# First batch element: second-layer results leave PSUM by ScalarE and are added by GpSimd, its output is sent in parts, and x's first products go ahead of its second half's transposes

## The chip, the cores and the metric

The kernel runs on one core of a Trainium2 chip. The metric is the device time of one execution in microseconds, the median of three runs; the profile is one more execution with the hardware profiler. Five engines work side by side, each in the order of its own instruction stream: TensorE (PE) multiplies, VectorE (DVE), ScalarE (ACT) and GpSimd (POOL) do elementwise work, SyncE (SP) issues DMA transfers. Semaphores connect them: an instruction that waits for another engine holds up everything behind it on its own engine. Matrix products land in PSUM banks; here a pool of two banks ("M") takes the products of the MLP part, a pool of four ("S") the attention scores.

## What is computed

Attention with normalized queries and keys, and its output, head by head side by side, goes through an MLP mixer. There are eight batch elements, 12 heads of 64, 448 positions, so x is 448 x 768 for each element.

```python
def _attn_ref(q, k, v, g_q, g_k):
    def rmsnorm(x, g):
        rms = np.sqrt(np.mean(x * x, axis=-1, keepdims=True) + 1e-06)
        return x / rms * g
    q_n, k_n = (rmsnorm(q, g_q), rmsnorm(k, g_k))
    scores = np.matmul(q_n, k_n.transpose(0, 1, 3, 2)) / np.sqrt(q.shape[-1])
    attn = np.exp(scores - np.max(scores, axis=-1, keepdims=True))
    attn = attn / (np.sum(attn, axis=-1, keepdims=True) + 1e-09)
    return np.matmul(attn, v)

def _moe_ref(x, w_tok1, w_tok2, w_ch1, w_ch2):
    xt = x.transpose(0, 2, 1)
    h = np.maximum(xt @ w_tok1, 0.0) @ w_tok2      # token mixing, 448 -> 256 -> 448
    u = x + h.transpose(0, 2, 1)
    h2 = np.maximum(u @ w_ch1, 0.0) @ w_ch2        # channel mixing, 768 -> 1536 -> 768
    return u + h2
# x = attention's output, (B,H,S,D) -> (B,S,H*D)
```

## The kernel before

The core works through the batch elements one after the other. While PE does the MLP of element b, the attention of element b + 1 is woven between its products, so PE always has two streams. Element 0 is special in its channel mixing. For the elements after it, the kernel uses seven products of half-size blocks instead of eight (Strassen's way), and needs sums of weight blocks for that. For element 0 the weights are only just being read from memory and converted, so it uses plain products, stage by stage, as the converted chunks come: 18 stages of the first layer, then 18 of the second (three output groups m = 2, 0, 1 of six stages each). The sums of weight blocks are made at the same time on GpSimd and written back to device memory (`ws`), to be read as "units" later. Each weight chunk takes four DVE operations, one ACT operation and two loads.

The stage of element 0's channel mixing:

```python
def first_stage(n):
    w, _, m, t = stages[n]
    wide = w is moe_w_ch2                       # second layer
    last = (KF if wide else KC) - 1
    if t == 0:
        st["m", 0], st["m", 1] = m_tile(), m_tile()        # both banks of pool M
    a, u = st.pop(("stage", n)), st["uT", 0]
    for o in range(2):
        ps = st["m", o][:, 0:S]
        for half in range(2):
            nc.tensor.matmul(out=ps, lhsT=a[:, o + 2 * half, :],                  # L781
                rhs=natural(half)[:, :, t, :] if wide else u[:, half * KC + t, :],
                start=(t == 0 and half == 0), stop=(t == last and half == 1))
        if t < last:
            continue
        if wide:
            to = u[:, o * KC + m, :]
            nc.vector.tensor_tensor(out=to, in0=to, in1=ps, op=ALU.add)           # L789
        else:
            nc.scalar.activation(out=natural(o)[:, :, m, :], ..., func=AF.Relu)
```

The matrix u is held transposed (`uT`). A result leaves by a DVE transpose of 32 x 32 blocks into one of four buffers, and four DMA transfers from SyncE's queue:

```python
turn_pool = pool("turn_pool", 4)

def trans_y(b, cc):
    t = st["y", cc] = turn_pool.tile([P, S], F32, name="turned")
    nc.vector.transpose(out=t[:], in_=st["uT", b][:, cc, :])                      # L900

def turns(b, cs, send=True):
    def one(cc):
        trans_y(b, cc)
        if send:
            later(2.0, lambda: send_y(b, cc, st.pop(("y", cc))))
    return [(0.3, lambda cc=cc: one(cc)) for cc in cs]

def y_order(b):        # for b = 0: 2, 5, 0, 3, 1, 4
    return [o * KC + m for m in ((0, 1, 2) if b else (2, 0, 1)) for o in range(2)]
```

`later` puts a piece of work a given number of (planned) microseconds further back in program order. Numbers such as 0.3 are weights by which `merge` weaves lists of work into one order; they are no measured times.

x of element 0 is turned by PE itself (`x_items`, L663, and an ACT copy, L665); `tok1` is the first product of token mixing on one half of x (L685, then `h`, L688), `tok2` the second (L693, then a DVE add into uT, L698). For later elements x goes through device memory: DVE transposes (L671), transfers to `xs` (L639) and back (L646). The loop:

```python
for b in range(B):
    early, double = middle_items(b)
    if b == 0:
        early, last = first_items(x_items(0, 1) + tok1_items(0, 0) + tok1_items(0, 1) + early, double, some)
    else:
        if in_next(b - 1):                       # every b but the first
            y, z = sends(b - 1, y_order(b - 1)[:4]), left
            left = [y[0], y[1], z[0], y[2], z[1], y[3]]
        run(merge(tok1_items(b, 0), left[:2]))
        begin, early = merge(tok1_items(b, 1) + early[:3 * KC], left[2:]), early[3 * KC:]
        # [...]
    att = ...                                    # attention of element b + 1, x_items(b + 1, 0) within
    if b == 0:
        last = x_items(1, 1) + merge(
            last, direct + sums[:5], turns(b, y_order(b)[:4], not in_next(b)))
    else:
        # [...]
    run(merge(att, early) + last)
    if b == 0:
        load_units(0)
    left = turns(b, y_order(b)[4:])
```

So four of element 0's six results are turned after the last conversions and stay in the four buffers; they are sent in the course of element 1, between the turns of the last two. `sums` and `direct` are the weight sums on GpSimd (L205 to L208), with loads L241 and stores L212; `unit` loads are L740; L177 loads raw weights, L264 to L309 convert them (L275 on ACT).

Of the kernel before, what the change touches and what calls it, by code (L numbers as in the profile page):

```python
# [13 lines left out]
ALU = mybir.AluOpType  # L14
# [12 lines left out]
def merge(*lists):  # L27

    totals = [sum(c for c, _ in l) or 1.0 for l in lists]
    done = [0.0] * len(lists)  # L30
    at = [0] * len(lists)
    res = []
    while True:
        live = [i for i in range(len(lists)) if at[i] < len(lists[i])]
        if not live:
            return res
        i = min(live, key=lambda i: (done[i] + lists[i][at[i]][0] / 2) / totals[i])
        c, fn = lists[i][at[i]]
        at[i] += 1
        done[i] += c  # L40
        res.append((c, fn))
# [3 lines left out]
def whole(ctx, tc, shifted, pre, q, k, v, g_q, g_k, moe_w_tok1, moe_w_tok2, moe_w_ch1, moe_w_ch2, out):  # L45


    nc = tc.nc
# [18 lines left out]
    KC, KF = NC // 2, NF // 2  # L67
# [47 lines left out]
    def later(us, fn):  # L115

        at = clock[0] + us
        i = len(pending)
        while i and pending[i - 1][0] > at:
            i -= 1  # L120
        pending.insert(i, (at, fn))
# [190 lines left out]
    def weight_items(lo, hi):  # L312

        def one(i):
            if 3 <= i and i + 2 < len(chunks):
                weight_load(i + 2)
            convert_bits(i - 2)
            if i < len(chunks):
                convert_first(i)
            if 0 <= i - 1 < len(chunks):  # L320
                convert_second(i - 1)
            if 0 <= i - 2 < len(chunks):
                convert_last(i - 2)
            if 0 <= i - 3 - len(first):
                store(i - 3 - len(first))
        return [(1.0, lambda i=i: one(i)) for i in range(lo, hi)]
# [298 lines left out]
    def send_y(b, cc, t):  # L625

        dst = out[b][:, cc * P:(cc + 1) * P]
        for i in range(0, P, 32):
            (nc.sync if in_next(b) else nc.scalar).dma_start(
                out=dst[:, i:i + 32].rearrange("(n t) c -> t n c", t=32),  # L630
                in_=t[i:i + 32].rearrange("t (n c) -> t n c", c=32))
# [22 lines left out]
    def trans_x(b, j):  # L654

        half, o = divmod(j, KC)
        if b == 0:

            if o == 0:
                x_tile(b, half)  # L660
            ps = s_tile("t_ps")
            for c in range(NS):
                nc.tensor.transpose(  # L663
                    ps[0:R, c * P:(c + 1) * P], st["uT", b][:, j, c * R:(c + 1) * R], ident[:, :])
            nc.scalar.copy(  # L665
                out=st["x", b, half][0:R, o], in_=ps[0:R, :].rearrange("p (c n) -> p c n", c=NS))
            return

        if j == 0:
            st["xt"] = tu_pool.tile([P, 2, KC, S], F32, name="xt", tag="tu")  # L670
        nc.vector.transpose(out=st["xt"][:, half, o, :], in_=st["uT", b][:, j, :])  # L671
        if o == KC - 1:
            t = st["xt"][:, half].rearrange("p j s -> p (j s)")
            if half:
                st.pop("xt")
            later(2.0, lambda: send_x(b, half, t))
            later(12.0, lambda: load_x(b, half))

    def tok1(b, jc, h):
        cs = slice(h * HC, (h + 1) * HC)  # L680
        if h == 0:
            st["h1", jc] = h1_pool.tile([P, C], F32, name="h1", tag="h1")
        ps = m_tile()
        for c in range(NS):
            nc.tensor.matmul(  # L685
                out=ps[:, 0:HC], lhsT=w1_sb[0:R, c, jc * P:(jc + 1) * P], rhs=st["x", b, h][0:R, :, c, :],
                start=(c == 0), stop=(c == NS - 1))
        nc.scalar.activation(out=st["h1", jc][:, cs], in_=ps[:, 0:HC], func=AF.Relu)  # L688
# [63 lines left out]
    def r_tile(i):  # L752
        return r_pool.tile([P, 2 * HS], F32, name=f"r{i}")
# [12 lines left out]
    def natural(o):  # L766
        s = (HB["B11"], HB["T1"]) if o == 0 else (HB["B21"], HB["B22"])
        return hb[:, s[0]:s[1] + 1:s[1] - s[0]]

    def first_stage(n):  # L770

        w, _, m, t = stages[n]
        wide = w is moe_w_ch2
        last = (KF if wide else KC) - 1
        if t == 0:
            st["m", 0], st["m", 1] = m_tile(), m_tile()
# [4 lines that stand above are left out]
                nc.tensor.matmul(  # L781
                    out=ps, lhsT=a[:, o + 2 * half, :],
                    rhs=natural(half)[:, :, t, :] if wide else u[:, half * KC + t, :],
                    start=(t == 0 and half == 0), stop=(t == last and half == 1))
            if t < last:
                continue
            if wide:
                to = u[:, o * KC + m, :]
                nc.vector.tensor_tensor(out=to, in0=to, in1=ps, op=ALU.add)  # L789
            else:  # L790
                nc.scalar.activation(
                    out=natural(o)[:, :, m, :], in_=ps.rearrange("p (i n) -> p i n", i=2), func=AF.Relu)
        st["used"].add(("stage", n))
# [104 lines left out]
# [12 lines that stand above are left out]
    def y_order(b):  # L910

        return [o * KC + m for m in ((0, 1, 2) if b else (2, 0, 1)) for o in range(2)]

    def sends(b, cs):
        return [(0.3, lambda cc=cc: send_y(b, cc, st.pop(("y", cc)))) for cc in cs]
# [3 lines left out]
    def x_items(b, h):  # L919
        return [(0.1, lambda j=j: trans_x(b, j)) for j in range(h * NC // 2, (h + 1) * NC // 2)]  # L920

    def tok1_items(b, h):
        return [(us(NS, HC), lambda j=j, h=h: tok1(b, j, h)) for j in range(NJ)]
# [13 lines left out]
    def in_next(b):  # L937


        return b < B - 1 and not shifted  # L940

    def first_items(tok, prods, some):


        convert = weight_items(BEFORE, len(chunks) + 3)
        items = merge(tok, convert[:5])
        for j, it in enumerate(prods[:-6]):
            items.append(it)
            items += [(0.0, convert[5 + k][1]) for k in range(len(convert) - 5) if begins(k) == j]
            if j % 2 and j < 2 * len(some):  # L950
                items.append(some[j // 2])
        return items, prods[-6:]

    def begins(k):


        return 2 + -(-k * 14 // 10) if k < 10 else min(k + 7, 29)
# [30 lines left out]
    for p in (4, 5):  # L988
# [7 lines left out]
        out=g_t[:, 0:1], in0=g_t[:, 0:1], scalar=float(D) ** 0.5, in1=g_t[:, 1:2],  # L996
# [19 lines left out]
    for b in range(B):  # L1016
        early, double = middle_items(b)
        if b == 0:
            early, last = first_items(x_items(0, 1) + tok1_items(0, 0) + tok1_items(0, 1) + early, double, some)
        else:  # L1020
            if in_next(b - 1):

                y, z = sends(b - 1, y_order(b - 1)[:4]), left
                left = [y[0], y[1], z[0], y[2], z[1], y[3]]
            run(merge(tok1_items(b, 0), left[:2]))
            begin, early = merge(tok1_items(b, 1) + early[:3 * KC], left[2:]), early[3 * KC:]
            if b == 1:
                early, double = merge(begin + early, sums[5:20]), merge(double, sums[20:])
                begin = []
            early = begin + early + double  # L1030
            early, last = early[:-4], early[-4:]
        lo = (b + AHEAD) * per + 1
        att = []
        if b + AHEAD < B:
            att = att_items(lo, lo + 10) + x_items(b + AHEAD, 0) + att_items(lo + 10, lo + per)
        if b == 0:
            last = x_items(1, 1) + merge(
                last, direct + sums[:5], turns(b, y_order(b)[:4], not in_next(b)))
        else:
            if b + 1 < B:  # L1040
                last = merge(last, x_items(b + 1, 1))
            last += last_items(b)
# [4 lines that stand above are left out]
# [187 lines left out]
def kernel(  # L1234
# [33 lines left out]
    with arm.Else():  # L1268
        whole(tc, True, pre, *args)
# [30 lines left out]
```

## Time and profile before

| | |
|---|---|
| time, median of 3 (lowest to highest) | 1353.59 us (1351.46 to 1354.92) |
| span of the profiled execution | 1351.2 us |
| PE, DVE, ACT, POOL busy | 95%, 56%, 27%, 28% of the span |
| tok1 of element 1 begins, of element 2, of element 3 | 274.4, 443.7, 601.5 us |
| L781, matmuls of element 0's channel mixing | 288, 539 ns each as listed (they overlap) |
| L789, the add out of PSUM, 128 x 448 | 6, 612 ns each |
| L900, output turns, all elements | 48, 636 ns each |
| L629, output transfers | 192, 56 KB each |

The page gives the busy share of each engine in 40 slices, the costliest groups of instructions, and the chain of work that ended last. The timeline gives one line for each run of instructions on an engine: start and length in us, engine, source line, operation, output and input by the program's names, shape and count, and in brackets the idle time before it with what ended it. A DVE wait that no PE instruction ever meets costs nothing; idle time of PE is what adds to the span.

### The profile page before, as it was taken

Reading aid. Unit: us, or ns where it says so; the run is one execution under the profiler, and the core shown is the slowest. Engines: PE = TensorE matmul, PEld = TensorE weight load, DVE = VectorE, ACT = ScalarE, POOL = GpSimd, SP = SyncE. Lnnn points to the kernel's source line nnn. Section 1 sums busy time; section 2 is a strip of 40 time slices with the busy share of each in tenths; the row PEclk is TensorE's granted clock in tenths of the full one; section 3 lists DMA queues with packets and bytes.
Section 4 is the critical chain, followed back from the end, with each engine's and each line's share of the span. In section 5 each row is a group of like instructions: output and inputs, shape, how many; then the busy total and the mean of one; then the engine's idle time right before and its main releaser. Section 6 shows DMA issues by size and latency. Waiting matters only on the chain.

```text
span 1351.2 us, 20151 instructions
## 1 busy us (share of the span) xinstructions
PE 1284.4 (95%) x7408; PEld 925.0 (68%) x7408; DVE 753.5 (56%) x1295; ACT 366.2 (27%) x734; POOL 380.4 (28%) x443
## 2 busy tenths in 40 slices
PE   5989997979999999999999999999999999999997
PEld 3444443436778577795778757795777967787997
DVE  6878689626664455635655265644556365543212
ACT  5553432122330233203331223302332023300100
POOL 1201540336652232202231123312322034211220
PEclk9999998989999999999999999999999999999998
DMA  9655487889879566694559665594665955475554
GB/s 209 164 169 150 127 222 198 185 228 228 220 197 237 131 168 158 136 246 99 134 147 203 169 148 127 133 255 91 168 158 127 249 118 157 124 178 136 184 168 99
DMA packets 501521, 227.82 MB, mean 169 GB/s; under 512 B 373605, under 2 KB 463077, under 8 KB 501413
## 3 DMA queue, kind: packets, MB, share of 16 engines
q1 hardware_dynamic: 488290, 224.60, 67.4%
q10 hardware_dynamic: 12994, 1.84, 0.8%
q8 instruction: 61, 1.00, 0.3%
q14 instruction: 48, 0.39, 0.1%
q0 software_dynamic: 128, 0.00, 0.0%
HBM read 186.84 MB, written 39.52 MB: 168 GB/s over the span
## 4 chain that ended last, share of the span: by engine, by line
PE 76%; DVE 11%; DMA 5%; SPq 2%; ACT 2%; POOL 2%; issue 2%; DVEq 0%; ACTq 0%; POOLq 0%
PE m_ps L864 25%; PE m_ps L807 19%; PE o_ps L459 8%; PE s_ps L385 8%; PE m_ps L781 7%; PE m_ps L685 5%; PE m_ps L693 3%; DVE es L427 2%; DVE qk_t L350 2%; DMA unit<-ws 2%; PE d_ps L439 1%; ACT e L389 1%; DVE uT L698 1%; DVE qkT L365 1%; PE m_ps L439 1%
## 5 line engine op out<-in xcount | busy, mean ns | idle before, releaser
L864 PEld LDWEIGHTS m_ps<-hb,unit 128*128 128x128 f32 x1764 | 332.1, 190 | 14.8 <-issue 11.3
L864 PE MATMUL m_ps<-hb,unit 128*128 128x224 f32 x1764 | 339.5, 354 | 1.1 <-DMA unit<-ws 1.1
L807 PE MATMUL m_ps<-tu,unit 128*128 128x224 f32 x1008 | 202.8, 356 | 3.9 <-DVE r L812 3.8
L807 PEld LDWEIGHTS m_ps<-tu,unit 128*128 128x128 f32 x1008 | 188.3, 190 | 23.0 <-DVE r L812 6.2
L389 ACT ACTIVATE e<-s_ps 128x448 f32<-128x448 f32 x336 | 156.8, 547 | 99.7 <-PE s_ps L385 99.1
L807 PE MATMUL m_ps<-uT,unit 128*128 128x224 f32 x756 | 155.0, 357 | 6.3 <-ACT r L828 3.1
L807 PEld LDWEIGHTS m_ps<-uT,unit 128*128 128x128 f32 x756 | 140.4, 190 | 23.2 <-DVE uT L698 7.0
L459 PE MATMUL o_ps<-e,v 64*64 64x448 f32 x1316 | 149.4, 541 | 0.1
L385 PE MATMUL s_ps<-qkT 64*64 64x448 f32 x1260 | 145.1, 547 | 0.2 <-ACT qkT L368 0.2
L873 POOL TENSOR_TENSOR uT<-uT,r 128x448 f32<-128x448 f32 (+1 forms) x56 | 52.7, 951 | 263.3 <-DVE r L873 150.0
L812 DVE TENSOR_TENSOR r<-m_ps,r 128x448 f32<-128x448 f32 x63 | 39.0, 619 | 124.1 <-PE m_ps L807 64.5
L873 DVE TENSOR_TENSOR uT<-uT,m_ps 128x448 f32<-128x448 f32 (+1 forms) x70 | 34.0, 502 | 124.6 <-PE m_ps L864 124.6
L427 DVE TENSOR_TENSOR es<-es,e 128x896 f32<-128x896 f32 x84 | 93.0, 1107 | 14.5 <-ACT e L389 11.2
L459 PEld LDWEIGHTS o_ps<-e,v 64*64 64x64 f32 x1316 | 49.7, 133 | 69.7 <-issue 64.9
L812 POOL TENSOR_TENSOR hb<-r,r 128x448 f32<-128x448 f32 x21 | 27.9, 1326 | 239.6 <-ACT r L828 181.3
L385 PEld LDWEIGHTS s_ps<-qkT 64*64 64x64 f32 x1260 | 44.0, 132 | 70.0 <-issue 60.6
L693 PE MATMUL m_ps<-w_sb,h 128*128 128x448 f32 x192 | 79.9, 560 | 12.5 <-ACT h L688 7.1
L685 PE MATMUL m_ps<-x,w_sb 112*128 112x384 f32 x256 | 87.1, 494 | 0.0
L427 POOL TENSOR_TENSOR es<-e 128x896 f32<-128x896 f32 x21 | 43.9, 2088 | 138.5 <-ACT e L389 138.5
L368 ACT ACTIVATE qkT<-qkT,g_t 128x448 f32<-128x448 f32 x36 | 24.1, 668 | 210.7 <-DVE qkT L365 210.7
L685 PEld LDWEIGHTS m_ps<-x,w_sb 112*128 112x128 f32 x256 | 48.4, 192 | 36.4 <-ACT e L389 4.2
L693 PEld LDWEIGHTS m_ps<-w_sb,h 128*128 128x128 f32 x192 | 35.5, 194 | 53.8 <-issue 24.4
(116 smaller groups left out, 1381.4 us busy)
## 6 DMA issues: line engine op xcount, KB each, us to landing
unit<-ws SPq DMA_DIRECT2D x294, 384.0 KB, 4.0
raw<-in_moe_w_ch_dram SPq DMA_DIRECT2D x72, 256.0 KB, 3.5
v<-in_v_dram SPq DMA_DIRECT2D x94, 112.0 KB, 4.3
xs<-xt SPq DMA_DIRECT2D x56, 168.0 KB, 4.4
x<-xs SPq DMA_DIRECT2D x14, 672.0 KB, 6.8
out_dram<-turned SPq DMA_DIRECT2D x168, 56.0 KB, 2.0
qk_t<-in_q_dram SPq DMA_DIRECT2D x144, 56.0 KB, 3.0
qk_t<-in_k_dram SPq DMA_DIRECT2D x144, 56.0 KB, 3.4
```

Of the source, the lines that this page charges most:

```text
L350: nc.vector.tensor_tensor(out=x, in0=x, in1=r.unsqueeze(2).to_broadcast(list(x.shape)), op=ALU.mult)
L385: nc.tensor.matmul(out=pss[i][rows_of(i, a), 0:S], lhsT=qkT[h, 1, k * D:(k + 1) * D], rhs=qkT[h, 0, :], start=True, stop=True)
L389: nc.scalar.activation(out=e[:, i, :], in_=pss[i][:, 0:S], func=AF.Exp)
L427: eng.tensor_tensor(out=es[:], in0=(es if k > 1 else st["e", t, 0])[:], in1=st["e", t, k][:], op=ALU.add)
L459: nc.tensor.matmul(out=st["o", p][a * D:(a + 1) * D, 0:S], lhsT=vt[rows, k * D:(k + 1) * D], rhs=e[rows, :], **kw)
L685: nc.tensor.matmul(out=ps[:, 0:HC], lhsT=w1_sb[0:R, c, jc * P:(jc + 1) * P], rhs=st["x", b, h][0:R, :, c, :], start=(c == 0), stop=(c == N ...
L693: nc.tensor.matmul(out=ps[:, 0:S], lhsT=st["h1", jc][:, cc * P:(cc + 1) * P], rhs=w2_sb[:, jc].rearrange("p c r -> p (c r)"), start=(jc == ...
L781: nc.tensor.matmul(out=ps, lhsT=a[:, o + 2 * half, :], rhs=natural(half)[:, :, t, :] if wide else u[:, half * KC + t, :], start=(t == 0 an ...
L807: nc.tensor.matmul(out=ps[:, j * HS:(j + 1) * HS], lhsT=w[:, t, j, :], rhs=m, start=(t == 0), stop=(t == KC - 1))
L812: add = lambda e, o, x, y: e.tensor_tensor(out=o, in0=x, in1=y, op=ALU.add)
L864: nc.tensor.matmul(out=ps[:, j * HS:(j + 1) * HS], lhsT=st["w"](j, t), rhs=hb[:, HB[what], t, :], start=(t == 0), stop=(t == KF - 1))
L873: add = lambda e, o, x, y: e.tensor_tensor(out=o, in0=x, in1=y, op=ALU.add)
```

## The change

Three things, all in batch element 0. The six adds of the second layer's results, which read PSUM on DVE, become a copy on ACT out of PSUM (into buffers that later elements use for their block products) and an add on GpSimd from there. This is to give the two banks back without waiting for DVE, which is converting weights. The output is sent in parts: two results are turned and sent while the last stages still run, the next two behind them, and the last two as before at element 1's beginning, where no sends of the first four are left. This is to keep the four turn buffers free. And the first product of token mixing on x's first half goes ahead of the transposes of x's second half, which wait for the attention of later heads.

```diff
@@ first_stage
             if wide:
-                to = u[:, o * KC + m, :]
-                nc.vector.tensor_tensor(out=to, in0=to, in1=ps, op=ALU.add)
+                to, c = u[:, o * KC + m, :], r_tile(1 + o)[:]
+                nc.scalar.copy(out=c, in_=ps)
+                nc.gpsimd.tensor_tensor(out=to, in0=to, in1=c, op=ALU.add)
@@ first_items: the list of stages j, with their conversions
             if j % 2 and j < 2 * len(some):
                 items.append(some[j // 2])
+            if j in (26, 28):
+                items += turns(0, [y_order(0)[j // 2 - 13]])
@@ the loop over elements
         if b == 0:
-            early, last = first_items(x_items(0, 1) + tok1_items(0, 0) + tok1_items(0, 1) + early, double, some)
+            early, last = first_items(
+                tok1_items(0, 0) + x_items(0, 1) + tok1_items(0, 1) + early, double, some)
         else:
-            if in_next(b - 1):
+            if b > 1 and in_next(b - 1):
                 y, z = sends(b - 1, y_order(b - 1)[:4]), left
@@
         if b == 0:
-            last = x_items(1, 1) + merge(
-                last, direct + sums[:5], turns(b, y_order(b)[:4], not in_next(b)))
+            last = x_items(1, 1) + merge(last, direct + sums[:5], turns(b, y_order(b)[2:4]))
```

What it does to the order of instructions: on PE, one group of four transposes, the first product, eight scores, four values, the second product, then twelve transposes, instead of sixteen transposes first. The second layer's chunks are 18 to 35. On ACT, the first two copies stand behind the conversion step of chunk 29, the next two behind that of chunk 35, the last two behind one square more. On DVE, one turn stands just before chunk 35's conversion begins, one behind chunk 34's last step, then four in a row behind x's transposes for element 1. On GpSimd, four adds stand ahead of the six weight sums made straight from staged chunks, and two behind the second of the sums whose chunks are read back from device memory.

## The prediction, made before the run

> **What bounds the kernel now.** I read the page's slices first. TensorE (PE) is busy 95% of the span, so a change that touches only batch element 0 can win no more than the holes in PE's row:
>
> ```profile
> PE   5989997979999999999999999999999999999997
> ...
> DVE  6878689626664455635655265644556365543212
> ...
> DMA  9655487889879566694559665594665955475554
> ```
>
> A slice is 33.8 us. Counted from 0, the holes lie in slices 2, 6 and 8 (68 to 101, 203 to 236 and 270 to 304 us); after that PE is dense. In slice 6 VectorE (DVE) is at 9 tenths; in slice 8 it is at 2 and the DMA engines at 8. PE in order of time, around these holes (start, length, engine, line, operation; at the end the idle time and its releaser):
>
> ```profile
> 84.91 1.08 PE L663 MATMUL t_ps<-ident,uT 128*112 128x128 f32 x8
> 87.68 0.65 PE L663 MATMUL t_ps<-ident,uT 128*112 128x128 f32 x4 [1.68 <-DVE uT L505]
> 91.81 1.10 PE L663 MATMUL t_ps<-ident,uT 128*112 128x128 f32 x4 [3.49 <-DVE uT L505]
> 92.71 3.80 PE L685 MATMUL m_ps<-x,w_sb 112*128 112x384 f32 x8
> ...
> 217.83 6.28 PE L781 MATMUL m_ps<-hb,stage 128*128 128x448 f32 x16
> 231.63 7.83 PE L781 MATMUL m_ps<-hb,stage 128*128 128x448 f32 x16 [7.52 <-DVE uT L789]
> ...
> 256.28 18.31 PE L781 MATMUL m_ps<-hb,stage 128*128 128x448 f32 x48 [1.43 <-DVE uT L789]
> ...
> 299.36 6.59 PE L693 MATMUL m_ps<-w_sb,h 128*128 128x448 f32 x12 [7.14 <-ACT h L688]
> ```
>
> Four holes: A, 5.2 us, the transposes of x's second half wait for attention of the last head pairs; B, 7.5 us, and C, 1.4 us, the second layer's next output group waits until DVE has added the last one out of its two PSUM banks; D, 7.1 us, element 1's token mixing waits for a ScalarE (ACT) result. Each long hole costs more than its idle time: the 16 matmuls behind B take 7.83 against 6.28 us, the 8 behind A 3.80 against 2.85 at 98.86, and behind D the table of stretches shows a granted clock of 0.85 from 300 to 310, another 1.5 us. A to D are 21.2 us idle and about 4 us of slow matmuls.
>
> What DVE, ACT and SyncE do at B, C and D (their timelines):
>
> ```profile
> 225.91 2.28 DVE L427 TENSOR_TENSOR es<-es,e 128x896 f32<-128x896 f32 x2
> ...
> 230.96 1.14 DVE L789 TENSOR_TENSOR uT<-uT,m_ps 128x448 f32<-128x448 f32 x2
> ...
> 237.74 1.16 DVE L365 STREAM_TRANSPOSE qkT<-qk_t 128x448 f32<-128x448 f32 x2
> ...
> 241.93 0.43 DVE L264 TENSOR_SCALAR e_t<-raw 128x512 uint32<-128x512 uint32 x1 [2.46 <-DMA raw<-in_moe_w_ch_dram]
> ...
> 296.14 0.65 DVE L900 STREAM_TRANSPOSE turned<-uT 128x448 f32<-128x448 f32 x1 [20.89 <-DMA out_dram<-turned]
> ...
> 298.82 0.49 ACT L688 ACTIVATE h<-m_ps 128x384 f32<-128x384 f32 x1
> ...
> 287.86 7.73 SPq L629 DMA_DIRECT2D out_dram<-turned x8
> ```
>
> PE left the banks at 224.1, but DVE reached their two adds only at 230.96: it works a backlog of weight conversions. At D DVE stood still for 20.9 us: the fifth output turn needs one of four buffers, all held by results whose sending starts at 287.86. Behind that turn stand DVE's reduction (296.71), ACT's four small copies (297.78), `h` (298.82), then PE.
>
> **What the Trainium skill says.** "PSUM — Partial Sum Buffer", section The four PSUM rules: GpSimd has no access to PSUM. So the copy through ScalarE is forced; the trace has the same pair already, L816's copy (0.53 us) followed by L812's GpSimd add (1.13 us at 331.00). The same page, section Engine vs sequencer instructions, calls the queues of ScalarE, VectorE and GpSimd strict FIFO. D is that rule at work: nothing of DVE ran between 275.3 and 296.1. "TensorE: Matmul & The Clock Gate", section What's actually happening, says that the array falls to half clock after an idle window of about 3.4 us and needs about as long to return; 7.83 against 6.28 behind B agrees. "SBUF — State Buffer", section Who interferes with whom, says that a DVE instruction with two SBUF inputs contends with a GpSimd one that reads SBUF. The trace shows such stretching: a conversion step (L265) of 0.69 us takes 2.45 at 193.35, a GpSimd sum (L205) of 0.46 takes 1.30 at 313.56. GpSimd is idle from 200.2 to 244.2, though, so the first adds fall into empty time.
>
> **Part 1, x's order (A).** The new PE order has one transpose group, first product, 8 scores, values, second product, then the other three groups. The first product can start once x's copy (85.94, 0.59 us) is done: about 86.6, ending at 89.4; scores and values to 91.8; second product to 94.6; the transposes by then find their data (L505 done at 91.8) and end near 96.6. The next scores began at 101.63. Of the 5.0 us, some 0.8 go because a 1.05 us square stands ahead of the three copies that free score banks. Gain 4.2 us. DVE follows: its 4.2 us wait at 99.94 was for an ACT step queued behind scores that A had delayed. From 128 to 220 PE has no wait, and most DVE waits from 96 to 232 (the waits view: 8.7 us on ACT with this one, 6.3 on GpSimd) move with PE; 4.4 us are on DMA. I carry 4.0 us to B.
>
> **Part 2, copies instead of adds (B, C).** It takes 6 x 0.61 = 3.7 us off DVE, gives ACT 6 x 0.53 = 3.2 and GpSimd 6 x 1.13 = 6.8 us. In the old run's clock: ACT's copies follow its conversion step for stage 29, which needs DVE's L267 at 224.97 and stands behind four exponentials; the copies are done at 226.7 rather than the adds at 231.6, 4.9 us sooner. PE then does its two stages (6.2) and the values (1.7) by 234.6, and meets the next scores, which need the DVE transposes of 237.74. Those move up only by the two adds, 1.14 us: to 236.6, plus two transposes and ACT's scaling, 238.5. The old scores ran at 240.94, so 4.9 us have become 2.4. At C the copies stand behind ACT's step for stage 35. DVE gets to that through the raw load at 241.93, which is SyncE's and DMA's doing and does not move, and now has a turn of 0.6 us in front: 254.2 instead of 253.6. Step and copy: 255.6, against a resume at 256.28. The whole part is worth **0.7 us** in that place: a wait on banks becomes a wait on DVE's conversions.
>
> **Part 3, results sent early (D).** With two turns and their sends during the last stages, and two sends right behind, no turn finds the buffers full. The turn that stalled now waits for the last two GpSimd adds, which stand behind two weight sums. The old sums began at 280.24; I allow 1 us for sends that now lie ahead in SyncE's queue: 281.3, two sums of 1.76 to 284.8, two adds to 287.1, turns to 288.3, reduction 289.4, ACT's small copies 290.4, `h` at 290.9. PE comes there at 292.2 - 0.7 = 291.5, so no wait is left. Gain 7.1 plus 1.5 us of slow matmuls = 8.6. Against it: x's second half for element 1 (load issued 271.83, about 7.6 to land) arrived just before its use at 279.7. PE is now there 0.7 us sooner, while four send DMAs (224 KB in all) stand ahead of that load: 1.5 us of new wait.
>
> **Sum.** 4.0 + 0.7 + 8.6 - 1.5 = 11.8 us. Element 1 has the DMA engines at 89% of 274 to 444 us and 109% in 324 to 344, and has one wait for a weight unit (1.1 us at 432.29). With PE 12 us earlier I take 1 us off for another such wait. From element 2 on nothing is changed. 1353.6 - 10.8 = **1342.8 us**.
>
> **Rivals.** (1) The first-half gain is swallowed: DVE's conversions from 160 to 260 hang on raw loads that SyncE issues back to back from 180 to 203, so A's 4 us end in a longer wait at B. For it: DVE is busy 8.7 to 9.7 us of every 10 from 200 to 240. Against: those waits on DMA are only 4.4 us, and the loads themselves wait for DVE. Then 1346 to 1347. (2) The early sends delay the transfers of x or the weight sums, DMA being 84 to 101% busy from 260 to 280: the wait at D stays with another name, on GpSimd's adds or on x. Every us that the sums' reload slips beyond about 1.6 goes into the wait. Then 1347 to 1350; a loss needs slips of over 10 us. (3) All four holes close and stay closed: 21.2 + 4 us, some 1329. Against it stands the DVE chain of part 2, which bounds B whoever empties the banks.
>
> **Range and chances.** Rivals 1 and 2 together leave 3 to 5 us of gain; if DVE profits more than I carried, 16. So 1337 to 1349 for 8 in 10. Two per cent are 27 us, more than all the holes: faster by over 2% 0.01, within 2% 0.98, slower 0.01.
>
> **What would show it.** In the new trace: first product near 86.6 and scores near 97; the wait at B split into about 2.5 us on the ACT copy and about 4 us before the scores, on qkT; at C some wait on ACT left; no DVE wait on out_dram; the second tok1 half waiting 1 to 2 us for x; D gone. I am wrong if scores do not wait after B (then more is gained), if D's wait persists on uT from GpSimd, or if later PE waits on units sum to over 3 us.

## The result, and the profile after

The changed kernel takes 1345.62 us (median of 4 runs, 1343.76 to 1346.66), the kernel before on the same chip 1354.26 us (4 runs, 1351.46 to 1355.12). The ratio is 0.9938, with a 95% interval from 0.9919 to 0.9957: 8.6 us less.

In the page's slices of the changed kernel, TensorE's row shows the holes of slices 6 and 8 one digit shallower, not gone (a slice is now 33.6 us):

```profile
PE   5989998989999999999999999999999999999997
```

TensorE's timeline of the changed kernel, with the runs that answer to holes A to D (start, length, engine, line, operation; in brackets the idle time before it and its releaser):

```profile
84.95 2.85 PE L685 MATMUL m_ps<-x,w_sb 112*128 112x384 f32 x8 [1.02 <-ACT x L665]
...
99.41 1.99 PE L385 MATMUL s_ps<-qkT 64*64 64x448 f32 x10 [4.21 <-ACT x L665]
...
224.61 6.28 PE L781 MATMUL m_ps<-hb,stage 128*128 128x448 f32 x16 [1.62 <-ACT r L790]
...
238.07 1.01 PE L385 MATMUL s_ps<-qkT 64*64 64x448 f32 x2 [4.78 <-ACT qkT L368]
241.26 31.57 PE L781 MATMUL m_ps<-hb,stage 128*128 128x448 f32 x80
...
278.25 2.82 PE L685 MATMUL m_ps<-x,w_sb 112*128 112x384 f32 x8 [0.26 <-DMA x<-xs]
...
296.53 5.88 PE L693 MATMUL m_ps<-w_sb,h 128*128 128x448 f32 x8 [3.90 <-DVE uT L698]
```

Every hole but C has a successor. At A the transposes no longer wait (5.2 us before), but the next scores do, for 4.2 us, on an ACT copy. At B the banks come free early (1.6 us instead of 7.5), and the scores behind them wait 4.8 us. At D, 7.1 us on `h` have become 3.9 us on `uT` from L698, which is DVE's add of the previous token-mixing product.

To see where the time went I cut both traces at five events of the program: the first transpose of x's second half (L663), the first product of element 0's channel mixing (L781), element 1's first product (L685), its first block product with a unit (L807, in the changed kernel L809), and element 2's first product (L685).

| stretch | before, us | after, us | gain | holes in it |
|---|---|---|---|---|
| 84.91 to 128.08 (after: 83.28 to 126.96) | 43.2 | 43.7 | -0.5 | A |
| to 274.43 (272.66) | 146.3 | 145.7 | 0.6 | B, C |
| to 313.45 (308.62) | 39.0 | 36.0 | 3.1 | D |
| to 443.71 (435.39) | 130.3 | 126.8 | 3.5 | rest of element 1 |

These sum to 6.7 us. Another 1.6 us are there before the first changed instruction runs (83.28 against 84.91), so they come from the two executions and not from the change; below, profiles are therefore compared by stretches, and kernels by medians.

**A after.** ScalarE's timeline shows the copies that the scores wait for:

```profile
97.83 1.06 ACT L1170 ACTIVATE sq<-qk_t 112x1024 f32<-112x1024 f32 x1 [4.30 <-DVE ms L1187]
98.79 1.54 ACT L665 COPY x<-t_ps 112x512 f32<-112x512 f32 x3
```

They stand behind a square for the next query norm, and this waits 4.3 us for DVE's reduction L1187, because it writes the buffer that this reduction still has to read. DVE, and then GpSimd, at that time:

```profile
90.06 2.58 DVE L282 SCALAR_TENSOR_TENSOR raw<-raw,e_t 128x512 uint32<-128x512 uint32 x1
92.67 2.19 DVE L264 TENSOR_SCALAR e_t<-raw 128x512 uint32<-128x512 uint32 x1
...
96.57 1.23 DVE L1187 TENSOR_REDUCE ms<-sq 112x16 f32<-112x1040 f32 x1
```

```profile
89.80 2.28 POOL L427 TENSOR_TENSOR es<-e 128x896 f32<-128x896 f32 x1 [27.66 <-ACT e L389]
92.16 2.41 POOL L427 TENSOR_TENSOR es<-es,e 128x896 f32<-128x896 f32 x1
```

The two conversion steps ahead of the reduction, 0.70 and 0.43 us at 85.91 and 86.64, take 2.58 and 2.19 us beside GpSimd's two sums of exponentials. In the kernel before these sums ran behind the reduction (94.53), not in front of it: the earlier scores of part 1 brought them forward. GpSimd's timeline of the kernel before:

```profile
98.51 2.08 POOL L427 TENSOR_TENSOR es<-e 128x896 f32<-128x896 f32 x1 [36.40 <-ACT e L389]
```

**B after.** GpSimd's two adds at B, and below them what DVE does beside them (a chunk takes five DVE operations, L264, L265, L267, L282 and L309, not four):

```profile
224.63 2.82 POOL L791 TENSOR_TENSOR uT<-uT,r 128x448 f32<-128x448 f32 x2 [25.52 <-ACT r L790]
```

```profile
224.84 1.62 DVE L282 SCALAR_TENSOR_TENSOR raw<-raw,e_t 128x512 uint32<-128x512 uint32 x1
226.50 1.24 DVE L264 TENSOR_SCALAR e_t<-raw 128x512 uint32<-128x512 uint32 x1
```

Elsewhere these two steps take 0.68 and 0.43 us. So the adds put on GpSimd cost DVE 1.75 us at this place and save it 1.14 us, and it is DVE that the scores behind B wait for. From chunk 29's step L267 to the end of the two transposes L365 DVE takes 14.4 us, against 13.9 before (222.89 to 237.32; 224.97 to 238.90). Counted from the beginning of its stretch in the table above, TensorE is back at the second layer's products (L781, 241.26 and 242.56) only 0.2 us sooner.

**D after.** DVE's timeline, from the first of the last two turns to L698, and below it GpSimd's:

```profile
285.17 0.65 DVE L902 STREAM_TRANSPOSE turned<-uT 128x448 f32<-128x448 f32 x1 [23.65 <-POOL uT L791]
...
288.96 1.17 DVE L1204 SCALAR_TENSOR_TENSOR ms<-ms,half 128x56 f32<-128x56 f32 x1 [1.08 <-ACT half L1195]
...
291.94 1.99 DVE L1228 SCALAR_TENSOR_TENSOR nt<-rs 128x56 f32<-128x56 f32 x1
...
295.86 1.14 DVE L698 TENSOR_TENSOR uT<-uT,m_ps 128x448 f32<-128x448 f32 x2
```

```profile
280.45 0.46 POOL L205 TENSOR_TENSOR raw<-raw 128x128 f32<-128x128 f32 x1 [12.40 <-DMA raw<-ws]
...
284.01 2.23 POOL L791 TENSOR_TENSOR uT<-uT,r 128x448 f32<-128x448 f32 x2
...
291.79 2.07 POOL L427 TENSOR_TENSOR es<-es,e 128x896 f32<-128x896 f32 x1
```

DVE no longer stands still for a buffer. It stands still for the two GpSimd adds (284.01), and these stand behind two weight sums that are read back from memory. After the turns come eleven small steps of the query norm (Newton's iteration for the root, L1204 to L1230). Before, with GpSimd idle, they ran from 298.83 to 301.53, 2.7 us; now from 288.96 to 295.95, 7.0 us, with GpSimd at work beside them. The kernel before, DVE and GpSimd:

```profile
298.83 0.22 DVE L1199 SCALAR_TENSOR_TENSOR ms<-ms,half 128x56 f32<-128x56 f32 x1 [1.08 <-ACT half L1190]
```

```profile
303.46 1.44 POOL L716 TENSOR_TENSOR tu<-uT 128x224 f32<-128x224 f32 x1 [10.25 <-DVE uT L698]
```

### The profile page after: what moved, and what is told of

The parts are those of the page before. It is cut to its first block, busy times and chain, and to the rows that moved or that the text cites. A ratio compares the mean times of both kernels' runs of the same rounds, so it can differ in the third digit from the quotient of the medians.

```text
span 1343.4 us, 20171 instructions
## 1 busy us (share of the span) xinstructions
PE 1284.4 (96%) x7408; PEld 926.5 (69%) x7408; DVE 757.2 (56%) x1289; ACT 368.7 (27%) x740; POOL 385.1 (29%) x449
## 4 chain that ended last, share of the span: by engine, by line
PE 72%; DVE 15%; DMA 4%; POOL 3%; issue 2%; ACT 2%; SPq 1%; DVEq 0%; ACTq 0%; POOLq 0%
PE m_ps L866 25%; PE m_ps L809 19%; PE o_ps L459 7%; PE s_ps L385 7%; PE m_ps L685 5%; PE m_ps L693 4%; DVE es L427 2%; DVE qk_t L350 2%; DMA raw<-in_moe_w_ch_dram 1%; DVE raw L265 1%; DVE raw L282 1%; PE m_ps L781 1%; PE d_ps L439 1%; ACT e L389 1%; DMA unit<-ws 1%
## 5 line engine op out<-in xcount | busy, mean ns | idle before, releaser
L809 PE MATMUL m_ps<-tu,unit 128*128 128x224 f32 x1008 | 202.6, 355 | 3.8 <-DVE r L814 3.8
L809 PEld LDWEIGHTS m_ps<-tu,unit 128*128 128x128 f32 x1008 | 188.4, 190 | 21.8 <-DVE r L814 7.0
L809 PE MATMUL m_ps<-uT,unit 128*128 128x224 f32 x756 | 154.6, 357 | 6.1 <-ACT r L830 2.5
L385 PE MATMUL s_ps<-qkT 64*64 64x448 f32 x1260 | 147.9, 551 | 9.0 <-ACT qkT L368 4.8
L809 PEld LDWEIGHTS m_ps<-uT,unit 128*128 128x128 f32 x756 | 140.6, 190 | 22.8 <-DVE uT L698 5.7
L693 PE MATMUL m_ps<-w_sb,h 128*128 128x448 f32 x192 | 80.6, 564 | 7.7 <-DVE uT L698 7.7
L685 PE MATMUL m_ps<-x,w_sb 112*128 112x384 f32 x256 | 86.4, 490 | 1.3 <-ACT x L665 1.0
L427 POOL TENSOR_TENSOR es<-e 128x896 f32<-128x896 f32 x21 | 44.1, 2101 | 131.8 <-ACT e L389 131.8
L685 PEld LDWEIGHTS m_ps<-x,w_sb 112*128 112x128 f32 x256 | 47.8, 190 | 37.7 <-ACT e L389 4.2
L1187 DVE TENSOR_REDUCE ms<-sq 128x28 f32<-128x896 f32 (+2 forms) x45 | 48.7, 1084 | 44.4 <-ACT sq L1173 41.8
```

The source lines that it names most:

```text
L385: nc.tensor.matmul(out=pss[i][rows_of(i, a), 0:S], lhsT=qkT[h, 1, k * D:(k + 1) * D], rhs=qkT[h, 0, :], start=True, stop=True)
L427: eng.tensor_tensor(out=es[:], in0=(es if k > 1 else st["e", t, 0])[:], in1=st["e", t, k][:], op=ALU.add)
L685: nc.tensor.matmul(out=ps[:, 0:HC], lhsT=w1_sb[0:R, c, jc * P:(jc + 1) * P], rhs=st["x", b, h][0:R, :, c, :], start=(c == 0), stop=(c == N ...
L693: nc.tensor.matmul(out=ps[:, 0:S], lhsT=st["h1", jc][:, cc * P:(cc + 1) * P], rhs=w2_sb[:, jc].rearrange("p c r -> p (c r)"), start=(jc == ...
L809: nc.tensor.matmul(out=ps[:, j * HS:(j + 1) * HS], lhsT=w[:, t, j, :], rhs=m, start=(t == 0), stop=(t == KC - 1))
L1187: self.nc.vector.tensor_reduce(out=st["ms", p][:, p % 2, lo:hi], in_=sq[:, lo:hi], axis=AX_X, op=ALU.add)
```

## The experiments

Each kernel was timed together with the kernel before on the same chip. "Difference" is between the two medians. None leaves out work.

| kernel | us (runs) | before | difference | ratio, 95% interval |
|---|---|---|---|---|
| part 1 alone | 1352.38 (22) | 1352.43 | 0.0 | 0.9999, 0.9991 to 1.0008 |
| part 2 alone | 1354.23 (22) | 1352.43 | +1.8 | 1.0013, 1.0005 to 1.0021 |
| part 3 alone | 1341.13 (6) | 1352.43 | -11.3 | 0.9910, 0.9892 to 0.9927 |
| other buffers for two turns, nothing else | 1348.73 (9) | 1352.43 | -3.7 | 0.9966, 0.9953 to 0.9980 |
| the change, last two adds on DVE | 1341.48 (6) | 1352.77 | -11.3 | 0.9918, 0.9901 to 0.9936 |
| the change, fewer sums at the end of element 0 | 1346.05 (6) | 1352.77 | -6.7 | 0.9950, 0.9933 to 0.9967 |
| part 1 and a square buffer of its own | 1349.79 (18) | 1352.77 | -3.0 | 0.9975, 0.9965 to 0.9985 |
| parts 1 and 3 and that buffer | 1337.21 (6) | 1352.77 | -15.6 | 0.9887, 0.9869 to 0.9904 |
| parts 2 and 3 | 1345.13 (6) | 1353.12 | -8.0 | 0.9945, 0.9925 to 0.9965 |
| the change and that buffer | 1340.37 (6) | 1353.12 | -12.8 | 0.9917, 0.9895 to 0.9938 |

The stretches of the table above, in their profiles:

| kernel | A | B, C | D | rest of element 1 |
|---|---|---|---|---|
| before | 43.2 | 146.3 | 39.0 | 130.3 |
| the change | 43.7 | 145.7 | 36.0 | 126.8 |
| part 1 alone | 44.4 | 146.9 | 37.3 | 130.3 |
| part 2 alone | 43.4 | 144.2 | 39.6 | 130.6 |
| part 3 alone | 43.5 | 145.6 | 29.6 | 127.0 |
| other buffers | 43.2 | 145.0 | 30.9 | 134.5 |
| last two adds on DVE | 43.5 | 145.6 | 30.6 | 126.8 |
| fewer sums | 44.1 | 145.7 | 29.4 | 132.6 |
| part 1, own buffer | 40.2 | 145.5 | 39.6 | 129.9 |
| parts 1 and 3, own buffer | 40.4 | 145.6 | 29.2 | 128.1 |
| parts 2 and 3 | 43.4 | 146.0 | 33.8 | 126.5 |
| the change, own buffer | 40.2 | 145.7 | 33.5 | 126.9 |

### Part 1 alone

```diff
-            early, last = first_items(x_items(0, 1) + tok1_items(0, 0) + tok1_items(0, 1) + early, double, some)
+            early, last = first_items(
+                tok1_items(0, 0) + x_items(0, 1) + tok1_items(0, 1) + early, double, some)
```

> The kernel before with part 1 alone (x's first products ahead of its second half's transposes). Theory 1 (the hole only moves: the scores behind the transposes wait for x's copies on ScalarE, which stand behind a square that waits for a VectorE reduction, itself slowed by GpSimd's sums): 0 to 1 us gained, and a wait of about 4 us at the scores near 95 us. Theory 2 (the prediction's: some 4 us gained there and carried on): 1350 us or less, that is 3 to 5 us below before.

It is worth nothing: 1352.38 against 1352.43 us, within 0.1% either way. The hole is not swallowed further on; it never closes. TensorE's timeline of this kernel shows the same wait as in the whole change:

```profile
100.90 2.50 PE L385 MATMUL s_ps<-qkT 64*64 64x448 f32 x10 [4.23 <-ACT x L665]
```

### Part 2 alone

```diff
-                to = u[:, o * KC + m, :]
-                nc.vector.tensor_tensor(out=to, in0=to, in1=ps, op=ALU.add)
+                to, c = u[:, o * KC + m, :], r_tile(1 + o)[:]
+                nc.scalar.copy(out=c, in_=ps)
+                nc.gpsimd.tensor_tensor(out=to, in0=to, in1=c, op=ALU.add)
```

> The kernel before with part 2 alone (copies on ScalarE, adds on GpSimd). Theory 1 (VectorE's conversions bound this place whoever empties the banks, and the wait for the turn buffers stays): 0 to 2 us gained; the 7.5 us wait on the banks splits into about 2 us on the copy and about 4 us on qkT; the 7 us wait on h stays. Theory 2 (the banks were the bound): 6 to 10 us gained.

It loses 1.8 us. In TensorE's timeline the hole B is split in two and D is what it was:

```profile
227.22 7.98 PE L781 MATMUL m_ps<-hb,stage 128*128 128x448 f32 x16 [2.73 <-ACT r L789]
...
240.82 0.59 PE L385 MATMUL s_ps<-qkT 64*64 64x448 f32 x2 [3.21 <-ACT qkT L368]
...
298.14 7.53 PE L693 MATMUL m_ps<-w_sb,h 128*128 128x448 f32 x12 [7.10 <-ACT h L688]
```

2.7 and 3.2 us make 5.9 of the 7.5 us that were there, as they would if DVE's conversions set the time of the scores whoever empties the banks. In its profile the B, C stretch is even 2.1 us shorter than before and D 0.6 longer. The profiled execution took 1352.49 us, less than the median of 1354.23, and the loss that the medians show is in none of its stretches. The cause stays open.

### Part 3 alone

```diff
+            if j in (26, 28):
+                items += turns(0, [y_order(0)[j // 2 - 13]])
...
-            if in_next(b - 1):
+            if b > 1 and in_next(b - 1):
...
-            last = x_items(1, 1) + merge(
-                last, direct + sums[:5], turns(b, y_order(b)[:4], not in_next(b)))
+            last = x_items(1, 1) + merge(last, direct + sums[:5], turns(b, y_order(b)[2:4]))
```

> The kernel before with part 3 alone (turns and sends early, adds still on VectorE). Theory 1 (this part carries the gain): 5 to 9 us gained, the VectorE wait on out_dram of 20.9 us gone, the wait on h gone or under 2 us; since the last turns do not wait for GpSimd here, it may gain as much as the whole change or more. Theory 2 (the parts are worth something only together): under 3 us.

Part 3 alone gains 11.3 us, more than the whole change. D is as good as gone, in TensorE's timeline, and DVE's says why:

```profile
294.45 3.27 PE L693 MATMUL m_ps<-w_sb,h 128*128 128x448 f32 x8 [0.68 <-DVE uT L698]
```

```profile
275.05 1.16 DVE L900 STREAM_TRANSPOSE turned<-uT 128x448 f32<-128x448 f32 x2
...
289.05 2.04 DVE L1224 SCALAR_TENSOR_TENSOR nt<-rs 128x56 f32<-128x56 f32 x1
```

The last two turns run at 275.05, straight behind DVE's own adds, and not at 285.17 behind GpSimd's. The norm's steps are stretched here too (2.04 us for one), but counted from element 1's first product (274.31; in the changed kernel 272.66) they begin 2.6 us earlier, and the wait before L693 is 0.7 us instead of 3.9. D falls from 39.0 to 29.6 us, the rest of element 1 from 130.3 to 127.0.

### Other buffers for two turns

```diff
-        t = st["y", cc] = turn_pool.tile([P, S], F32, name="turned")
+        if b == 0 and cc in (1, 4):
+            t = st["y", cc] = r_tile(3 if cc == 1 else 5)
+        else:
+            t = st["y", cc] = turn_pool.tile([P, S], F32, name="turned")
```

> The kernel before with only this: element 0's last two turns go into two buffers that are free at that time (those of the block products r3 and r5), so no turn waits for a send; sends and their places are unchanged. Theory 1 (it was the lack of buffers that held VectorE, not the lateness of the sends as such): 5 to 9 us gained, like part 3. Theory 2 (sending early matters as such, since it takes 8 us of issue from SyncE's queue in element 1's first 25 us): at most half of what part 3 gains.

This parts the two things that part 3 does: here no turn waits for a buffer, but all 24 sends stay in element 1. D falls to 30.9 us, nearly as with part 3, so the full buffers were the cause of D, as theory 1 has it. Only 3.7 us remain in the time, which is what theory 2 expected, because the rest of element 1 takes 134.5 us, 7.5 more than with part 3. TensorE's timeline has new waits there:

```profile
338.60 2.54 PE L807 MATMUL m_ps<-tu,unit 128*128 128x224 f32 x12 [0.92 <-ACT r L816]
...
343.01 4.15 PE L807 MATMUL m_ps<-tu,unit 128*128 128x224 f32 x12 [1.88 <-DVE hb L812]
```

The two borrowed buffers are ones that element 1's block products use, but both waits lead back to a late load. On ScalarE a square waits 8 us for a part of k, where with part 3 alone it waits 2.0:

```profile
334.43 0.95 ACT L1171 ACTIVATE sq<-qk_t 128x896 f32<-128x896 f32 x1 [7.96 <-DMA qk_t<-in_k_dram]
```

The copy L816 stands behind this square on ScalarE, and on DVE the add L812 stands behind the norm steps that need its result. SyncE's queue issued the last of these loads at 330.11, with part 3 alone at 324.28, though TensorE begins its block products at almost the same time in both (303.74 and 303.94). In between it issues 16 sends here (8.9 us, from 297.21), with part 3 alone none after 297.6. The profile names no wait for the sends out of the borrowed buffers. So it is the crowd of sends that these two waits point to; how much of the 7.5 us it explains is not shown.

That part 3 helps the rest of element 1 is seen in the other rows too: 126.5 to 128.1 us in the kernels with part 3, 129.9 to 130.6 in those without it and without borrowed buffers, the kernel with fewer sums (below) apart. These rows alone do not tell the early sends from the time that DVE no longer loses at D.

### The change, with the last two adds on DVE

Group m = 1, the last of the three, is added out of PSUM on DVE again; the other two keep the copy.

```diff
-                to, c = u[:, o * KC + m, :], r_tile(1 + o)[:]
-                nc.scalar.copy(out=c, in_=ps)
-                nc.gpsimd.tensor_tensor(out=to, in0=to, in1=c, op=ALU.add)
+                to, c = u[:, o * KC + m, :], r_tile(1 + o)[:] if m != 1 else None
+                if m == 1:
+                    nc.vector.tensor_tensor(out=to, in0=to, in1=ps, op=ALU.add)
+                else:
+                    nc.scalar.copy(out=c, in_=ps)
+                    nc.gpsimd.tensor_tensor(out=to, in0=to, in1=c, op=ALU.add)
```

> The changed kernel, but the last output group (m = 1) is added on VectorE straight from PSUM, as before. Theory 1 (the change loses against part 3 alone because its last two turns wait for GpSimd adds that stand behind two weight sums, which puts the Newton steps of the next pair later): 1340 to 1342 us, 3 to 5 us below the changed kernel's 1345.6; the last two turns run near 274 us. Theory 2 (the loss comes from the earlier adds or from x's order): 1344 us or more.

Two adds on another engine turn a gain of 8.6 into one of 11.3 us. In DVE's and in TensorE's timeline the turns are back at 275 and the wait at D is down from 3.9 to 1.6 us:

```profile
274.77 1.16 DVE L905 STREAM_TRANSPOSE turned<-uT 128x448 f32<-128x448 f32 x2
```

```profile
295.11 3.27 PE L693 MATMUL m_ps<-w_sb,h 128*128 128x448 f32 x8 [1.61 <-DVE uT L698]
```

D takes 30.6 us instead of 36.0. So what the change loses at D against part 3 alone comes from these two adds: the turns, and the norm behind them, wait for GpSimd.

### The change, with fewer sums at the end of element 0

```diff
-                early, double = merge(begin + early, sums[5:20]), merge(double, sums[20:])
+                early, double = merge(begin + early, sums[3:20]), merge(double, sums[20:])
...
-            last = x_items(1, 1) + merge(last, direct + sums[:5], turns(b, y_order(b)[2:4]))
+            last = x_items(1, 1) + merge(last, direct + sums[:3], turns(b, y_order(b)[2:4]))
```

> The changed kernel, but two fewer of GpSimd's weight sums stand at the end of element 0 (they move into element 1's list). Theory 1 (VectorE's small Newton steps after the late turns are stretched from 2.7 to 7.0 us because GpSimd runs sums at that time): the steps take under 4 us, the 3.9 us wait of PE on the add out of its bank shrinks to under 1.5 us, 1342 to 1344 us. Theory 2 (the steps are late only because the turns are late): the wait stays above 3 us and the time at 1345 us or more.

The other way to free the last adds: here they stay on GpSimd but no longer stand behind read-back sums (they run at 272.46 and 273.97). The norm steps take 4.5 us, the wait at D falls to 0.28 us and the stretch to 29.4; the time does not, 6.7 us under before where the whole change is 8.6 under. TensorE's timeline shows what took it:

```profile
422.21 12.97 PE L866 MATMUL m_ps<-hb,unit 128*128 128x224 f32 x60 [3.81 <-DMA unit<-ws]
```

A unit comes late: SyncE issues the group of loads that ends this wait 116.3 us behind the end of stretch D (418.74, 302.46), in the changed kernel 111.5 us behind it (420.16, 308.62). The two weight sums more in element 1 are all that differs; the chain from them to this load is not traced. The rest of element 1 grows from 126.8 to 132.6 us. The expectation of less time was wrong, though the wait that it was about went away.

### Part 1 with a buffer of its own for the square

The edit to part 1 gives the square that held up the copies another buffer; nothing else differs.

```diff
-            sq = (self.sq_1 if p in (1, 3) else self.sq_2 if p in (5, 7) else self.sq)[0:rows]
+            sq = (self.sq_1 if p in (1, 3) else self.sq_2 if p in (5, 7, 9) else self.sq)[0:rows]
```

> The kernel before with x's order changed as in part 1, and the square that stands ahead of x's copies given a buffer of its own, so that it no longer waits for VectorE's reduction. Theory 1 (that wait is what kept part 1 from gaining): the 4.2 us wait at the scores is under 1 us. Then either the gain carries on (1348 to 1350 us), or the conversions on VectorE swallow it (the wait at the second layer's banks grows from 7.5 to about 10 us, and 1351 to 1353 us remain). Theory 2 (the copies are late for another reason): the wait at the scores stays above 3 us.

3.0 us less. In ScalarE's timeline the square (now written to `hb`) and the copies run as soon as their turn comes, and in TensorE's the next product of token mixing starts at 99.78 instead of 104.80, while B stays:

```profile
94.82 1.05 ACT L1166 ACTIVATE hb<-qk_t 112x1024 f32<-112x1024 f32 x1
95.77 1.55 ACT L665 COPY x<-t_ps 112x512 f32<-112x512 f32 x3
```

```profile
99.78 5.43 PE L685 MATMUL m_ps<-x,w_sb 112*128 112x384 f32 x16
...
228.59 7.84 PE L781 MATMUL m_ps<-hb,stage 128*128 128x448 f32 x16 [7.63 <-DVE uT L789]
```

DVE's conversion steps are still stretched (2.57 and 2.20 us at 91.46 and 94.06), and TensorE no longer meets them. So the shared buffer was the link that made A move instead of close. The gain is also there at the end: B does not grow from it (7.63 against 7.52 us), which speaks against rival 1 of the prediction.

### Parts 2 and 3, and the change with that buffer

Parts 2 and 3 without part 1; and the whole change with the line above.

> The changed kernel without part 1 (x in the old order; parts 2 and 3 stay). Theory 1 (part 1 is worth nothing, because the 4 us wait only moves from the first product to the scores; part 2 costs about 4 us next to part 3, because the last two turns then wait for GpSimd's adds): within 1.5 us of the changed kernel, so about 1345, and some 4 us above the 1341 of part 3 alone; the wait on DVE uT L698 before L693 at about 297 us stays near 4 us. Theory 2 (part 1 is what disturbs part 3, by moving everything behind it against the fixed transfers): about 1341, like part 3 alone, and the wait at L693 below 1.5 us.

> The changed kernel with a buffer of its own for the x square at p=9, so that ScalarE's copies for the scores no longer stand behind a square that waits for DVE's reduction. Theory 1 (the lost 4 us of part 1 are that shared buffer, and the gain carries on): the wait of the scores on ACT x L665 falls from 4.2 to under 1.5 us, the first element's first token stage ends some 4 us earlier (about 100 instead of 104.5), and the time is about 1342, 3 to 4 us under the changed kernel. Theory 2 (in the changed kernel a later wait takes it back, the banks or the last turns): the scores' wait goes, but the time stays within 1 us of the changed kernel's 1345, with the wait on qkT or on uT L698 longer by as much.

Parts 2 and 3 come out at -8.0 us, the whole change at -8.6: in combination, too, part 1 as it was made is worth nothing that these runs can tell. Against part 3 alone, part 2 costs 3.3 us by the differences, 4.7 us by the ratios (0.0035 of 1353). The wait at D is much that of the whole change (3.4 us against 3.9), and on DVE the turns stand behind the same adds (285.37):

```profile
296.74 4.77 PE L693 MATMUL m_ps<-w_sb,h 128*128 128x448 f32 x8 [3.36 <-DVE uT L698]
```

The whole change with the buffer gains 12.8 us, 4.1 more than without it, and its stretch A is 40.2 us instead of 43.7. So A's gain carries on there too, as the first theory said.

### Parts 1 and 3 with that buffer: the best version

> Parts 1 and 3 of the change without part 2 (adds on VectorE), with the square's own buffer. If the two gains add: 1337 to 1339 us. If VectorE's conversions swallow the early one: 1341 us, the same as part 3 alone.

1337.21 us, 15.6 under before and below both kernels. The two gains add (3.0 and 11.3 make 14.3), and D has next to no wait left in TensorE's timeline:

```profile
289.04 3.27 PE L693 MATMUL m_ps<-w_sb,h 128*128 128x448 f32 x8 [0.28 <-DVE uT L698]
```

Hole B stays in it, 6.2 us: nothing tried here closes it.

## Why the prediction was right, and where it was not

The total was right, 10.8 us predicted and 8.6 measured, but much of that is luck. By the stretches the terms for A and D were 4.5 and 4.0 us too high and the one for later waits 4.5 us too low. The stretches add up to 6.7 us in the two traces; the 8.6 are from the medians.

**Part 1, predicted 4.0 us, found about 0.** The first product started where it was put (86.42 in part 1 alone, predicted about 86.6). The step that failed is "Of the 5.0 us, some 0.8 go because a 1.05 us square stands ahead of the three copies that free score banks". I counted the square's own duration and not what the square waits for: DVE's last reduction out of the same buffer, 4.3 us. I had quoted the stretching of DVE beside GpSimd, and had not asked which GpSimd work earlier scores bring forward. The scores came at 100.90 in part 1 alone, not "near 97".

**Part 2 at B and C, predicted 0.7 us, found 0.6 in the whole change's trace, by luck.** The wait on the banks did become one on the ACT copy (predicted about 2.5, measured 1.6) and one of the scores on `qkT` (about 4, measured 4.8). But the step "Those move up only by the two adds, 1.14 us" failed: the transposes did not move up, because GpSimd's adds stretch DVE's conversion steps by 1.75 us. That "the first adds fall into empty time" is true of GpSimd and not of DVE. At C no wait was left, where I had expected some. And the 0.6 us can't be put down to part 2: this stretch takes 145.0 to 146.9 us in the kernels that leave all adds on DVE, 144.2 to 146.0 in those with copies. Part 2 was not free elsewhere: by medians it costs 1.8 us alone and 3.3 beside part 3. (The copy ahead of the GpSimd add at 331.00 is L828's in the trace, not L816's; both take 0.53 us.)

**Part 3 at D, predicted 8.6 - 1.5 = 7.1 us, found 3.1 in the whole change.** The chain up to `h` was right within 0.5 us. Counted from element 1's first product (predicted 274.4 - 0.7 = 273.7, measured 272.66), the sums began at 7.8 us (predicted 7.6), the adds were done at 13.6 (13.4), the reduction at 15.2 (15.7) and `h` at 16.8 (17.2). x's second half waited 0.26, not 1.5 us. The step that failed is "PE comes there at 292.2 - 0.7 = 291.5, so no wait is left". My chain ended with `h`, but the next products also need L698, and on DVE L698 stands behind eleven norm steps, which ran 7.0 us instead of 2.7 because GpSimd's sums ran beside them. Had the turns not waited for GpSimd's adds, as in part 3 alone, D would have gained 9.4 us.

**Later waits, predicted -1, found +3.5 us.** The step "I take 1 us off for another such wait" had the wrong sign. SyncE's queue spent 16.4 us of element 1 issuing output sends before (7.73 + 4.47 + 1.94 + 2.28), and 10.4 after (2.11 at 282.75 and 8.32 at 289.96), and the rest of element 1 went from 130.3 to 126.8 us. The unit wait of 1.1 us is gone. That part 3 causes the gain is shown by the kernels with and without it. That it does so by the shorter queue of sends is made likely by the kernel with other buffers, and not shown apart.

**Rivals.** Rival 2 had the mechanism at D half right (a wait stays there, on GpSimd's adds) but blamed DMA for it; the sums started within 0.3 us of my estimate, counted from element 1's first product. Rival 1 is refuted by the run with the buffer of its own. Rival 3's 25 us were out of reach as long as B stands; the best version has 15.6 of them.

## What to carry to other kernels

When a wait is to be moved out of the way, follow every engine that the waiting work passes, up to the next instruction of the bounding engine, and for each instruction ahead of it in the queue ask what that one waits for (buffers included), not only how long it lasts. Moving an add from a busy engine to an idle one pays only if nothing on the path then waits for that engine's older queue: here the first four adds could move without loss (and without a gain that shows), the last two could not. The engine that is relieved may pay as well, when the other engine's work stretches its own beside it: at B this took more than the adds had. And measure the parts of a change one by one: one of three carried everything, and one cost time.

## What the runs showed of the hardware that was not expected

A small DVE step that meets a GpSimd sum is not slowed in proportion; it ends when the sum ends. In the changed kernel the norm step of 0.22 us at 291.94 ends at 293.93, GpSimd's sum of 291.79 at 293.86; the step at 288.96 meets a sum in its middle and ends at 290.13, the sum at 290.06. In part 3 alone the step at 289.05 ends at 291.09, GpSimd's sum of 288.93 at 291.02:

```profile
288.93 2.09 POOL L427 TENSOR_TENSOR es<-es,e 128x896 f32<-128x896 f32 x1
```

Beside the short sums of 0.46 us the same steps take 0.38 to 0.50. The Trainium skill's "SBUF — State Buffer", section Who interferes with whom, describes an exclusive lock on the ports that DVE and GpSimd share, and says of DVE's two-port modes that the engine that comes second waits for the whole instruction of the other; these pairs of ends agree with that. So a small DVE step beside a long GpSimd instruction took up to nine times its length here (1.99 against 0.22 us), and the chain of eleven steps 2.6 times (7.0 against 2.7 us).

The other surprise is how short a wait slows TensorE afterwards. The prediction went by about 3.4 us. In part 2 alone a wait of 2.73 us was enough: the granted clock is 0.50 from 229.2 to 231.2, and the 16 matmuls behind the wait take 7.98 us. Behind 1.62 us, in the changed kernel, the clock stays at 1.00 and 16 of the same take 6.28. Behind D's 3.9 us in the changed kernel it is 0.50 from 296.5 to 299.0, and eight matmuls take 5.88 us; behind 0.68 us, in part 3 alone, 3.27. So the slow matmuls at B are not gone in the changed kernel: behind the scores' wait of 4.8 us the clock is 0.50 from 238 to 242. Where between 1.6 and 2.7 us it begins, and whether that is fixed, no run here shows.
